# The head of a gated-mix kernel: x0's second half in token order, wk's first rows on SyncE's queue, ScalarE's loads behind its table load

## The chip, the core and the metric

One core of one Trainium2 chip. The metric is the device time of one execution in microseconds. The kernel before takes 261.64 us (median of 3 runs, 261.2 to 262.14).

## The reference, cut to what matters

x has 2048 tokens of 512 features in bf16. Two branches read it and a gate mixes them.

```python
x = A_x
g = _sigmoid((x * gate_w).sum(-1, keepdims=True))     # one gate value per token
a = _A_ref(x, A_wq, A_wk, A_wv, A_wo, A_beta)          # attention with a compressive memory
b = _B_ref(x, B_w_gate, B_w_up, B_w_down)              # gelu(x @ w_gate) * (x @ w_up) @ w_down
return g * a + (1 - g) * b
...
# _A_ref: 32 heads of 16 features, 4 segments of 512 tokens, in order
for s in range(N):
    qs, ks, vs = (q[:, :, s].copy(), k[:, :, s].copy(), v[:, :, s].copy())
    logits = jnp.einsum('bhqd,bhkd->bhqk', qs, ks) * scale + mask
    p = _softmax(logits, axis=-1)
    a_dot = jnp.einsum('bhqk,bhkd->bhqd', p, vs)
    ...
    o = g * a_mem + (1.0 - g) * a_dot
    ...
    M = M + jnp.einsum('bhld,bhle->bhde', pk, vs)
```

## The kernel before, in words

The four segments of 512 tokens are worked on one behind another, but their pieces are interleaved. Every piece is a task: a projection (K, Q, V), a block of attention, a tile of the gate (G), up (U) or down (D) products, an eviction, a DMA. The order of the tasks on each engine is written out by hand in ORDER (five strings, one for each of TensorE, ScalarE, VectorE, GpSimd and SyncE). A small planner, `Sched.schedule`, walks these orders with estimated durations. All that it decides is which of the four PSUM banks psW0 to psW3 a task takes; for the first loads it reads the estimated landing times from the table LANDING. `Emitter` then derives the semaphore waits from what each instruction reads and writes, and writes each engine's instructions in the order given.

The change lies in the head, before segment 0 can be projected.

- Segment 0's tokens come in two loads, x0_0 and x0_1, of 256 tokens each, into `xin` (four rows of 512 features in each partition; a part of the tile hT1, so the profile calls them hT). Before, both lay as "(p a) d": partition p holds tokens 2p and 2p+1 of the half, which are neighbours in memory, so each partition's piece is one run of 2 KB.
- wk, wq and wv are cut into pieces of rows: wk0 and wk1 (128 rows, 128 KB each), wk2 (256 rows, 256 KB), wq0, wq1, wv0 and wv1 (256 rows each). SyncE issues x0_0, x0_1, wk2, wq1, wv1, then wg0 (the first half of w_gate, 896 KB), and segment 1's transposing loads x1_0 to x1_3 with the gate's weights gwb and beta among them. ScalarE issues wk0, wk1, wq0 and wv0. They stand in its order behind `tload`, a one-element exponential which makes the table of functions load.
- TensorE begins with seven warm-up matmuls `warm0` to `warm6` of 512 columns, whose results nobody reads. Then come the transposes of x0_0 (`x0t0a_0`, `x0t0c_0`, `x0t0b_0`, `x0t1_0`: eight matmuls of 128 columns against an identity, into PSUM), evicted to `xT[0]` by VectorE and ScalarE (`x0ev...`). The K projection is cut into eight matmuls of 256 columns for each of four tiles: `.0` reads wk0 and the first half of the tokens, `.1` wk1 and the first half, `.2` and `.3` the same weights and the second half, `.4` to `.7` wk2. The order on TensorE is: transposes of x0_0, the four `.0`, transposes of x0_1, the four `.1`, then `.2`, `.3`, `.4` and so on; then the Q projection of segment 0 (16 matmuls of 512 columns), the last three of K, and the first tiles of G, which need wg0.
- The evictions of the transposes undo the token order: with tokens 2p and 2p+1 in partition p, the copy writes every second column of `xT[0]`.
- The gate of segment 0: `gmul0` multiplies `xin` by gwb on VectorE, `gsum0_0` to `gsum0_3` sum each row over the 512 features into columns 12 to 15 of `glog`, and four small DMAs on SyncE, `gl00` to `gl11`, move them to where each token's value belongs in columns 0 to 3, since the tokens' order in `xin` isn't that of the output tiles. `gexs0` on ScalarE takes the exponential of columns 0 to 3.

Of the kernel before, what the change touches and what calls it, by code (L numbers as in the profile page):

```python
# [13 lines left out]
ALU = mybir.AluOpType  # L14
# [24 lines left out]
LANDING = {  # L39
    "x0_0": 3.8, "w_wk0": 4.15, "x0_1": 5.2, "w_wk1": 5.7, "w_wk2": 6.6, "w_wq0": 7.0, "w_wq1": 8.4, "w_wv0": 9.2,  # L40
    "w_wv1": 10.2, "w_wg0": 12.2, "x1_0": 12.9, "w_gwb": 13.2, "x1_1": 13.8, "w_beta": 14.1, "x1_2": 14.4, "x1_3": 14.8,
# [53 lines left out]
    "act": (  # L95
# [349 lines left out]
def mm_t(n):  # L445
    return max(0.026, n / 2363.0)
# [19 lines left out]
def _build(es, nc, A_x, A_wq, A_wk, A_wv, A_wo, A_beta, B_w_gate, B_w_up, B_w_down, gate_w, out):  # L466
# [71 lines left out]
    def task(name, eng, instrs, **kw):  # L538
        return S.add(Task(name, {eng: instrs}, **kw))
# [55 lines left out]
    def wdma(key, eng, dst, src, nbytes, nonc=False, issue=0.5, reads=()):  # L595
        rank[0] -= 20000.0 if rank[0] > 1.0e5 else 20.0
        dma("w_" + str(key), eng, lambda: dst, lambda: src, list(reads), [("w", key)], nbytes, bias=rank[0],
            nonc=nonc, issue=issue)
# [25 lines left out]
    for u in range(2):  # L624
        rank[0] -= 20000.0
        dma(f"x0_{u}", SP, lambda u=u: xin[:, 2 * u:2 * u + 2, :],
            lambda u=u: A_x[0, u * 256:(u + 1) * 256, :].rearrange("(p a) d -> p a d", p=P), [],
            [("hT", 1, 2 * u + a) for a in range(2)], 250000, bias=rank[0], issue=0.5)
        for wkey, i, dst, src in wloads[u:u + 1] if u == 0 else wloads[1:]:
            wdma((wkey, i), SP if (wkey, i) in (("wk", 2), ("wq", 1), ("wv", 1)) else ACT, dst, src, 250000,  # L630
                 issue=0.5)
    wdma(("wg", 0), SP, wg[:, :, 0:half], wgr[:, :, 0:half], 790000)
# [7 lines left out]
    for i in range(7):  # L640
        gw = Grp(banks)
        task(f"warm{i}", PE, [Instr(lambda e, gw=gw: e.matmul(
            gw.f32()[:, :], ones[:, 0:128], ones[:, :], start=True, stop=True),
            [], [gw.key], mm_t(512))], grp=gw, bias=5000.0 - i)
    XB = XALL.bitcast(BF)
    for nm, u, k0, nk, c0, aa in (("0a", 0, 0, 1, 0, (0,)), ("0c", 0, 0, 1, 3584, (1,)), ("0b", 0, 1, 1, 1024, (0, 1)),
# [9 lines left out]
            for k in range(nk) for i, a in enumerate(aa)])  # L656
        dst = xT[0][:, k0:k0 + nk, 256 * u:256 * u + 256].rearrange("p k (c a) -> p k a c", a=2)[:, :, aa[0]:aa[-1] + 1, :]
        wr = [("xT", 0, k0 + k, u) if na == 2 else ("xT", 0, k0 + k, u, aa[0]) for k in range(nk)]
# [117 lines left out]
    def prep(s):  # L776
# [35 lines left out]
        if s > 0:  # L812
# [4 lines left out]
            ALU.mult), xkeys + [("w", "gwb")], xkeys, 1.32)])  # L817
        gl, gk = (glog[:, 12:16], ("glog", 3)) if s == 0 else (glog[:, s4], ("glog", s))
        for a in range(4):
            S.add(Task(f"gsum{s}_{a}", {  # L820
                ACT: [Instr(lambda e, a=a: e.activation(xt[:, a, :], xt[:, a, :], ACTF.Copy,
                                                        accum_out=gl[:, a:a + 1]),
                            [("gprod", s)] + xkeys, [gk + (a,), ("gjunk", s, a)], 0.64)],
                DVE: [Instr(lambda e, a=a: e.tensor_reduce(gl[:, a:a + 1], xt[:, a, :], AXX, ALU.add),
                            [("gprod", s)] + xkeys, [gk + (a,), ("gjunk", s, a)], dve_t(512))]}))
        if s == 0:
            for h in range(2):
                for a in range(2):
                    dma(f"gl{h}{a}", SP, lambda h=h, a=a: glog[a:P:2, h:4:2],
                        lambda h=h, a=a: glog[64 * h:64 * h + 64, 12 + a:16:2],  # L830
                        [gk + (c,) for c in (a, 2 + a)], [("glog", 0, h, a), ("glog", 0, 2 + h, a)], 60000, nonc=True)
        exp_task(ph, f"gexs{s}", [Instr(lambda e: e.activation(exs[:, s4], glog[:, s4], ACTF.Exp),
                                        [("glog", s, a) + u for a in range(4)
                                         for u in (((0,), (1,)) if s == 0 else ((),))], [("exs", s)], 0.25)])
        task(f"gts{s}", DVE, [
# [442 lines left out]
```

## Time and the profile before

| | |
|---|---|
| median of 3 runs | 261.64 us |
| the profiled execution's own time | 261.51 us |
| its span, first to last instruction | 260.3 us |
| granted TensorE clock over it | 1.00 |
| instructions | 10390 |
| DMA packets, bytes | 33100, 18.43 MB |
| HBM read, written | 9.84 MB, 2.10 MB |

The profile is one execution, taken by the hardware profiler. Times are microseconds from the start of the span unless they are marked ns. PE is TensorE's matmuls and PEld its weight loads, which overlap them; DVE is VectorE, ACT ScalarE, POOL GpSimd, SP SyncE. A name with a q behind it (SPq, ACTq) is that engine's sequencer issuing DMAs, which is not counted as busy time. Matmuls are pipelined and their ends are modelled, so a matmul's length is longer than the distance to the next one. A DMA's time to landing runs from its issue to the event that it has arrived. q1 is the queue that SyncE issues to, q10 the one of ScalarE. An arrow in brackets names what ended the idle time before an instruction. A share of the DMA engines over 1 means packets that overlap in time.

### The profile page before, as it was taken

How to read it: one execution, taken by the hardware profiler on the slowest of the kernel's cores; microseconds unless marked ns; L12 is line 12 of the kernel's file. 1: busy time of each engine (PE TensorE's matmuls, PEld its weight loads, DVE VectorE, ACT ScalarE, POOL GpSimd, SP SyncE). 2: the span in 40 equal slices, each digit the busy share in tenths (PEclk: the TensorE clock that was granted, in tenths of full speed). 3: DMA queues.
4: the chain of work that ended last, by engine and by line, in shares of the span. 5: the costliest groups of instructions: out<-in, count | busy, mean ns of one | idle time of the engine just before them, and what ended most of it. 6: DMA issues, size and time to landing. Idle time of an engine off the chain costs nothing.

```text
span 260.3 us, 10390 instructions
## 1 busy us (share of the span) xinstructions
PE 252.8 (97%) x4645; PEld 126.8 (49%) x4670; DVE 186.7 (72%) x346; ACT 211.3 (81%) x192; POOL 105.9 (41%) x260
## 2 busy tenths in 40 slices
PE   7999999999999999999999999999999999999996
PEld 3644445445554664534454563454455445454454
DVE  2398889998998338898987317889898602688574
ACT  4799999999998887979868967889985878777721
POOL 8216767814007264263810251445280044327320
DMA  7962212997013272070004023102001200420002
GB/s 220 309 180 42 59 30 59 252 358 149 3 23 61 44 106 63 12 115 3 3 4 102 4 63 73 33 4 87 0 6 23 81 5 0 108 61 3 3 3 83
DMA packets 33100, 18.43 MB, mean 71 GB/s; under 512 B 21152, under 2 KB 32800, under 8 KB 33056
## 3 DMA queue, kind: packets, MB, share of 16 engines
q1 hardware_dynamic: 32080, 16.96, 27.4%
q10 hardware_dynamic: 976, 0.82, 0.9%
q8 instruction: 36, 0.59, 0.9%
q14 instruction: 8, 0.07, 0.1%
HBM read 9.84 MB, written 2.10 MB: 46 GB/s over the span
## 4 chain that ended last, share of the span: by engine, by line
PE 92%; ACT 3%; DMA 2%; issue 2%; DVE 1%; SPq 0%; ACTq 0%
PE psW L544 33%; PE psW L546 25%; PE psW L1104 14%; PE psXALL L936 9%; PE psW L984 5%; DMA hT<-in_A_x_dram 2%; PE psXALL L546 2%; PE psW L992 1%; ACT ptl L942 1%; PE psXALL L544 1%; ACT pt L942 1%; PE psXALL L855 1%; PE psW L902 1%; DVE hT L1083 0%; PE psXALL L653 0%
## 5 line engine op out<-in xcount | busy, mean ns | idle before, releaser
L942 ACT ACTIVATE pt<-psXALL 128x2048 bf16<-128x2048 f32 x64 | 120.2, 1877 | 24.5 <-PE psXALL L936 23.5
L945 POOL TENSOR_SCALAR_AFFINE_SELECT pt<-pt 128x256 bf16<-128x256 bf16 x128 | 56.1, 448 | 90.1 <-ACT pt L942 85.3
L945 POOL TENSOR_SCALAR_AFFINE_SELECT ptl<-ptl 128x512 bf16<-128x512 bf16 x32 | 23.9, 747 | 48.6 <-ACT ptl L942 47.0
L1083 DVE TENSOR_TENSOR hT<-psW,hT 128x512 bf16<-128x512 f32 x56 | 37.2, 683 | 8.9 <-PE psW L544 6.7
L1104 PE MATMUL psW<-wd,hT 32*128 32x512 bf16 x576 | 35.0, 374 | 0.0
L544 PE MATMUL psW<-xT,wg 128*128 128x512 bf16 x121 | 29.8, 380 | 1.0 <-issue 0.6
L544 PE MATMUL psW<-xT,wu 128*128 128x512 bf16 x118 | 29.4, 380 | 1.3 <-issue 1.3
L998 DVE STREAM_TRANSPOSE tb<-psW 128x512 f32<-128x512 f32 x32 | 22.3, 705 | 8.7 <-PE psW L992 8.5
L936 PE MATMUL psXALL<-qT,kpad 32*128 32x320 bf16 (+3 forms) x512 | 25.6, 272 | 0.4 <-ACT ptl L942 0.2
L546 PE MATMUL psW<-xT,wu 128*32 128x512 bf16 x392 | 24.6, 380 | 0.0
L1133 DVE TENSOR_SCALAR ost<-psW,omgt 128x512 bf16<-128x512 f32 x11 | 8.0, 746 | 23.1 <-PE psW L544 21.9
L1104 PEld LDWEIGHTS psW<-wd,hT 32*128 32x128 bf16 x576 | 18.8, 93 | 10.6
L546 PE MATMUL psW<-xT,wg 128*32 128x512 bf16 x384 | 22.9, 380 | 0.0
L1067 ACT ACTIVATE hT<-psW 128x512 bf16<-128x512 f32 x28 | 15.5, 598 | 7.3 <-PE psW L546 7.1
L936 PEld LDWEIGHTS psXALL<-qT,kpad 32*128 32x128 bf16 x512 | 8.6, 92 | 22.7 <-ACT pt L942 15.9
L984 PE MATMUL psW<-pt,vaug 128*17 128x192 bf16 (+3 forms) x512 | 19.3, 273 | 0.0
L544 PEld LDWEIGHTS psW<-xT,wg 128*128 128x128 bf16 x128 | 11.5, 98 | 14.5 <-issue 1.5
L544 PEld LDWEIGHTS psW<-xT,wu 128*128 128x128 bf16 x126 | 11.2, 98 | 14.3 <-issue 2.1
L984 PEld LDWEIGHTS psW<-pt,vaug 128*17 128x17 bf16 x512 | 12.3, 91 | 10.0 <-issue 0.6
L942 ACT ACTIVATE ptl<-psXALL 128x2048 bf16<-128x2048 f32 x8 | 15.0, 1877 | 1.6 <-PE psXALL L936 1.6
L842 POOL COPY exsT<-exs 32x4 f32<-32x4 f32 x64 | 14.0, 219 | 3.8
L546 PEld LDWEIGHTS psW<-xT,wu 128*32 128x32 bf16 x392 | 10.1, 97 | 9.5 <-issue 0.8
(126 smaller groups left out, 379.8 us busy)
## 6 DMA issues: line engine op xcount, KB each, us to landing
out_dram<-ost SPq DMA_DIRECT2D x15, 128.0 KB, 1.8
wg<-in_B_w_gate_dram SPq DMA_DIRECT2D x2, 896.0 KB, 7.7
wu<-in_B_w_up_dram SPq DMA_DIRECT2D x2, 896.0 KB, 6.7
wd<-in_B_w_down_dram SPq DMA_DIRECT2D x2, 896.0 KB, 7.2
phkt<-in_A_x_dram SPq DMA_DIRECT2D x3, 512.0 KB, 3.9
vlow<-vaug SPq DMA_DIRECT2D x8, 136.0 KB, 2.7
hT<-in_A_x_dram SPq DMA_DIRECT2D x2, 256.0 KB, 3.6
wo<-in_A_wo_dram SPq DMA_DIRECT2D x1, 512.0 KB, 5.6
```

What stands on the lines that cost most here:

```text
L544: return e.matmul(view(), lhsT, rhs, start=first, stop=last)
L546: r = e.matmul(view()[c:c + 32, :], lhsT[:, c:c + 32], rhs, start=first, stop=last, tile_position=(0, c))
L842: cross = task(f"exsT{s}", POOL, [Instr(lambda e, g=g, c=c: e.tensor_copy(exsT[sl][32 * g:32 * g + 32, c:16:4], exs[32 * c:32 * c + 32, s4 ...
L936: instrs.append(Instr(lambda e, g=g, lhs=lhs, rhs=rhs, c0=c0, ncol=ncol: e.matmul(X[g][:, c0:c0 + ncol], lhs(32 * g), rhs(32 * g), start=T ...
L942: exp_task(s, f"exp{s}_{t}{name}", [Instr(lambda e: e.activation(dst[:], XALL[:, :].rearrange("p (g c) -> p g c", g=4), ACTF.Exp, scale=AT ...
L945: task(f"msk{s}_{t}{name}", POOL, [Instr(lambda e, view=view, pat=pat, base=base: e.affine_select(out=view, in_=view, compare_op=ALU.is_ge ...
L984: instrs.append(Instr(lambda e, t=t, q=q, kb=kb, slot=slot, c0=c0: e.matmul(gp.f32()[32 * q:32 * q + 17, 128 * kb + 64:512], Vaug[sl][:, k ...
L998: task(f"pvt{s}_{t}_{j}", DVE, [Instr(lambda e: e.transpose(Tb[:, j, :], gp.f32()[:, :]), [gp.key], [("Tb", j)], 0.71)], grp=gp)
L1067: lambda e, g=g, ft=ft, s=s: e.activation(hT[s % 2][:, ft, :], g.f32()[:, :], ACTF.Gelu_apprx_tanh),
L1083: task(f"Um{s}_{ft}", DVE, [Instr(lambda e, g=g, ft=ft: e.tensor_tensor(hT[sl][:, ft, :], g.f32()[:, :], hT[sl][:, ft, :], ALU.mult), [g.k ...
L1104: return Instr(lambda e: e.matmul(gs[tile].f32()[:, :], a[32 * r:32 * r + 32, :], b[32 * r:32 * r + 32, :], start=False, stop=False, tile_ ...
L1133: DVE: [Instr(lambda e: e.tensor_scalar(ost[:], g.f32()[:, :], omgt[:, gt:gt + 1], None, ALU.mult), rd, wr, dve_t(512, ap=True))]}, grp=g))
```

## The change

Six edits, and with them the line numbers behind them move by up to three.

- x0_1 is laid out as "(a p) d": partition p holds tokens p and 128 + p of the half. They aren't neighbours in memory, so each partition's piece is two runs of 1 KB. x0_0 stays as it was.
- The evictions of x0_1's transposes therefore write whole runs of columns of `xT[0]`, no longer every second one.
- wk0 moves from ScalarE's order to SyncE's, between x0_0 and x0_1.
- wk1, wq0 and wv0, still on ScalarE, now read the word that `tload` writes, so the first of them waits until `tload` is done and the two behind it follow.
- `warm6` has 128 columns instead of 512.
- The gate's sums for x0_1's tokens go straight into columns 2 and 3 of `glog`. The four small moves remain, but each takes one column instead of two and waits for one sum instead of two.

The estimated landing times in LANDING are set anew too; the PSUM banks that the planner gives out come out the same, and so does the order of everything else.

```diff
     "act": (
-        "tload w_wk0 w_wk1 w_wq0 w_wv0 x0ev0c_0 x0ev0b_0 x0ev0b_1 x0ev1_1 K0_0even K0_1ev K0_2ev kl0_01 pke0_0 Q0_1ev "
+        "tload w_wk1 w_wq0 w_wv0 x0ev0c_0 x0ev0b_0 x0ev0b_1 x0ev1_1 K0_0even K0_1ev K0_2ev kl0_01 pke0_0 Q0_1ev "
...
     "sp": (
-        "x0_0 x0_1 w_wk2 w_wq1 w_wv1 w_wg0 x1_0 w_gwb x1_1 w_beta x1_2 x1_3 w_wg1 gl00 gl11 Vlo0_1 gl10 gl01 pkT0_1 "
+        "x0_0 w_wk0 x0_1 w_wk2 w_wq1 w_wv1 w_wg0 x1_0 w_gwb x1_1 w_beta x1_2 x1_3 w_wg1 gl00 gl11 Vlo0_1 gl10 gl01 "
...
         dma(f"x0_{u}", SP, lambda u=u: xin[:, 2 * u:2 * u + 2, :],
-            lambda u=u: A_x[0, u * 256:(u + 1) * 256, :].rearrange("(p a) d -> p a d", p=P), [],
+            lambda u=u: A_x[0, u * 256:(u + 1) * 256, :].rearrange(("(p a) d -> p a d", "(a p) d -> p a d")[u], p=P), [],
             [("hT", 1, 2 * u + a) for a in range(2)], 250000, bias=rank[0], issue=0.5)
         for wkey, i, dst, src in wloads[u:u + 1] if u == 0 else wloads[1:]:
-            wdma((wkey, i), SP if (wkey, i) in (("wk", 2), ("wq", 1), ("wv", 1)) else ACT, dst, src, 250000,
-                 issue=0.5)
+            late = (wkey, i) in (("wk", 1), ("wq", 0), ("wv", 0))
+            wdma((wkey, i), ACT if late else SP, dst, src, 250000, issue=0.5, reads=[("stmp",)] if late else ())
...
     for i in range(7):
         gw = Grp(banks)
-        task(f"warm{i}", PE, [Instr(lambda e, gw=gw: e.matmul(
-            gw.f32()[:, :], ones[:, 0:128], ones[:, :], start=True, stop=True),
-            [], [gw.key], mm_t(512))], grp=gw, bias=5000.0 - i)
+        n = 128 if i == 6 else 512
+        task(f"warm{i}", PE, [Instr(lambda e, gw=gw, n=n: e.matmul(
+            gw.f32()[:, 0:n], ones[:, 0:128], ones[:, 0:n], start=True, stop=True),
+            [], [gw.key], mm_t(n))], grp=gw, bias=5000.0 - i)
...
-        dst = xT[0][:, k0:k0 + nk, 256 * u:256 * u + 256].rearrange("p k (c a) -> p k a c", a=2)[:, :, aa[0]:aa[-1] + 1, :]
+        dst = xT[0][:, k0:k0 + nk, 256 * u:256 * u + 256].rearrange(
+            ("p k (c a) -> p k a c", "p k (a c) -> p k a c")[u], a=2)[:, :, aa[0]:aa[-1] + 1, :]
...
-        gl, gk = (glog[:, 12:16], ("glog", 3)) if s == 0 else (glog[:, s4], ("glog", s))
+        col = [12, 13, 2, 3] if s == 0 else [4 * s + a for a in range(4)]
+        gks = [("glog", c // 4, c % 4) for c in col]
...
-                    dma(f"gl{h}{a}", SP, lambda h=h, a=a: glog[a:P:2, h:4:2],
-                        lambda h=h, a=a: glog[64 * h:64 * h + 64, 12 + a:16:2],
-                        [gk + (c,) for c in (a, 2 + a)], [("glog", 0, h, a), ("glog", 0, 2 + h, a)], 60000, nonc=True)
+                    dma(f"gl{h}{a}", SP, lambda h=h, a=a: glog[a:P:2, h:h + 1],
+                        lambda h=h, a=a: glog[64 * h:64 * h + 64, 12 + a:13 + a],
+                        [gks[a]], [("glog", 0, h, a)], 60000, nonc=True)
```

More of the change, by code (lines that the diff above doesn't have):

```diff
@@ L39 @@
 LANDING = {
-    "x0_0": 3.8, "w_wk0": 4.15, "x0_1": 5.2, "w_wk1": 5.7, "w_wk2": 6.6, "w_wq0": 7.0, "w_wq1": 8.4, "w_wv0": 9.2,
+    "x0_0": 3.5, "w_wk0": 3.85, "x0_1": 4.65, "w_wk1": 4.6, "w_wk2": 5.7, "w_wq0": 6.3, "w_wq1": 7.6, "w_wv0": 8.4,
     "w_wv1": 10.2, "w_wg0": 12.2, "x1_0": 12.9, "w_gwb": 13.2, "x1_1": 13.8, "w_beta": 14.1, "x1_2": 14.4, "x1_3": 14.8,
@@ L821, in prep @@
                 ACT: [Instr(lambda e, a=a: e.activation(xt[:, a, :], xt[:, a, :], ACTF.Copy,
[L822 to L825, printed above, removed]
+                                                        accum_out=glog[:, col[a]:col[a] + 1]),
+                            [("gprod", s)] + xkeys, [gks[a], ("gjunk", s, a)], 0.64)],
+                DVE: [Instr(lambda e, a=a: e.tensor_reduce(glog[:, col[a]:col[a] + 1], xt[:, a, :], AXX, ALU.add),
+                            [("gprod", s)] + xkeys, [gks[a], ("gjunk", s, a)], dve_t(512))]}))
         if s == 0:
@@ L828, in prep @@
                 for a in range(2):
-                    dma(f"gl{h}{a}", SP, lambda h=h, a=a: glog[a:P:2, h:4:2],
-                        lambda h=h, a=a: glog[64 * h:64 * h + 64, 12 + a:16:2],
-                        [gk + (c,) for c in (a, 2 + a)], [("glog", 0, h, a), ("glog", 0, 2 + h, a)], 60000, nonc=True)
+                    dma(f"gl{h}{a}", SP, lambda h=h, a=a: glog[a:P:2, h:h + 1],
+                        lambda h=h, a=a: glog[64 * h:64 * h + 64, 12 + a:13 + a],
+                        [gks[a]], [("glog", 0, h, a)], 60000, nonc=True)
         exp_task(ph, f"gexs{s}", [Instr(lambda e: e.activation(exs[:, s4], glog[:, s4], ACTF.Exp),
                                         [("glog", s, a) + u for a in range(4)
-                                         for u in (((0,), (1,)) if s == 0 else ((),))], [("exs", s)], 0.25)])
+                                         for u in (((0,), (1,)) if (s, a) in ((0, 0), (0, 1)) else ((),))], [("exs", s)], 0.25)])
         task(f"gts{s}", DVE, [
```

6 rows, old and new, of the table ORDER are left out of this document.

## The prediction

> **What bounds the kernel now.** I read the page first, for the engine that sets the end.
>
> ```profile
> span 260.3 us, 10390 instructions
> PE 252.8 (97%) x4645; PEld 126.8 (49%) x4670; DVE 186.7 (72%) x346; ACT 211.3 (81%) x192; POOL 105.9 (41%) x260
> PE 92%; ACT 3%; DMA 2%; issue 2%; DVE 1%; SPq 0%; ACTq 0%
> ```
>
> TensorE is busy for 97% of the span and is 92% of the chain that ended last. So the change, which touches only the head, is worth what it moves TensorE's stream there, if nothing later takes it back. Then I read the chain of waits over the first 16 us (start, length, what).
>
> ```profile
> 1.27 4.26 DMA hT<-in_A_x_dram
> 5.53 0.05 issue
> 5.57 0.62 PE psXALL L653 x8
> 6.19 2.73 PE psW L544 x25
> 8.97 3.40 PE psXALL L544 x15
> 12.38 1.19 PE psW L544 x7
> ```
>
> The DMA is x0_1, x's second 256 tokens: issued at 1.27, landed at 5.53. From 5.57 on, the chain is TensorE almost without a break. Next the timeline of the head (start, length, engine, line; in brackets the idle time before it and what ended it), with the warm-up's group of the by-shape view behind it.
>
> ```profile
> 0.81 1.28 ACT L617 ACT_TABLE_LOAD   x1 [0.81 <-PEq L1263]
> 0.85 3.15 PE L642 MATMUL psW<-const-bfloat16-1.0 128*128 128x512 bf16 x7 [0.85 <-PEq L1263]
> 0.87 0.89 ACTq L581 DMA_DIRECT2D wk<-in_A_wk_dram  x2
> 1.72 0.43 SPq L581 DMA_DIRECT2D wk<-in_A_wk_dram  x1
> 2.10 0.20 ACT L617 ACTIVATE stmp<-const-bfloat16-1.0 128x1 f32<-128x1 bf16 x1
> 3.82 0.47 PEld L653 LDWEIGHTS psXALL<-ident,hT 128*128 128x128 bf16 x8 [0.73 <-DMA hT<-in_A_x_dram]
> 3.83 0.64 PE L653 MATMUL psXALL<-ident,hT 128*128 128x128 bf16 x8
> 4.58 0.60 PE L544 MATMUL psW<-xT,wk 128*128 128x256 bf16 x4
> 5.57 0.62 PE L653 MATMUL psXALL<-ident,hT 128*128 128x128 bf16 x8 [0.40 <-DMA hT<-in_A_x_dram]
> 5.90 0.45 DVE L661 COPY xT<-psXALL 128x256 bf16<-128x256 bf16 x1 [0.66 <-PE psXALL L653]
> 5.98 2.67 PEld L544 LDWEIGHTS psW<-xT,wk 128*128 128x128 bf16 x25
> 12.43 0.64 PEld L544 LDWEIGHTS psW<-xT,wg 128*128 128x128 bf16 x4
> ...
> L642 PE MATMUL psW<-const-bfloat16-1.0 128*128 128x512 bf16 x7 | 3.1, 625 | 0.9 <-PEq L1263 0.9
> ```
>
> There are two gates. The first transposes start at 3.83, when two things end together: the seven warm-up matmuls (six steps of (3.15 - 0.625)/6 = 0.42 us, so the last starts at 3.37 and is through the array by about 3.80) and x0_0's landing. The second transposes wait 0.40 us for x0_1. Last I read the DMA view, for the landings (us from issue, one row of each load's own window) and for the packets.
>
> ```profile
> hT<-in_A_x_dram SPq DMA_DIRECT2D x1, 256.0 KB, 3.0
> wk<-in_A_wk_dram ACTq DMA_DIRECT2D x1, 128.0 KB, 3.2
> ...
> hT<-in_A_x_dram SPq DMA_DIRECT2D x1, 256.0 KB, 4.3
> ...
> wk<-in_A_wk_dram SPq DMA_DIRECT2D x1, 256.0 KB, 5.0
> wk<-in_A_wk_dram ACTq DMA_DIRECT2D x1, 128.0 KB, 4.5
> ...
> wg<-in_B_w_gate_dram SPq DMA_DIRECT2D x1, 896.0 KB, 9.0
> ```
>
> So x0_0 lands at 0.81 + 3.0 = 3.8, wk0 at 4.1, wk1 (issued about 1.3) at 5.8, wk2 at 6.7, and wg0, issued at 3.22, at 12.2. The packets of SyncE's queue (q1) and ScalarE's (q10), as packets, MB and share of the 16 engines, from 1.6 to 2.8, to 3.2 and to 4.4 us; then two stretches of the windows view, whose last figure is GB/s:
>
> ```profile
> q1 hardware_dynamic: 92, 0.19, 76.2%
> q10 hardware_dynamic: 2, 0.00, 0.5%
> ...
> q1 hardware_dynamic: 138, 0.26, 68.8%
> q10 hardware_dynamic: 64, 0.06, 11.5%
> ...
> q1 hardware_dynamic: 299, 0.53, 67.6%
> q10 hardware_dynamic: 251, 0.23, 24.2%
> ...
> 2.40:2.80 0.40, 0.40 (x2) 1.00 0.67 138
> 3.20:4.00 0.80, 0.80 (x5) 1.00 1.13 385
> ```
>
> ScalarE's wk0, issued at 0.87, has moved two packets by 2.8, though SyncE's x0_0, issued 0.06 us before it, has moved 92. And between 2.4 and 2.8 the engines move 138 GB/s where they move 385 soon after: x0_0 is running out and nothing else is there yet. That hole is worth 0.4 x (1 - 138/385) = 0.26 us of transfer.
>
> **The change, part by part.** *The seventh warm-up* shrinks from 512 to 128 columns: a quarter of 0.42, so TensorE is free at 3.37 + 0.11 = 3.48 instead of 3.80. That is 0.32 us at most, and only if x0_0 is there.
>
> *wk0 on SyncE's queue, ahead of x0_1.* SyncE now issues x0_0 at 0.81, wk0 at 1.27 and x0_1 at about 1.70, one issue (0.43) later than before; wk2, wq1, wv1, wg0 and the x1 loads slip by the same 0.43, but their data stands behind megabytes, so I cost the slip of the issues alone at nothing. In bytes the order up to x0_1's end stays: x0_0, wk0, x0_1, 640 KB. What goes is the hole. Also ScalarE's 0.06 MB no longer mixes into x0_0's end: 0.06 MB at 385 GB/s is 0.16 us. So x0_0 lands at 3.66 (bounds: 3.48, below which the warm-up rules, and 3.82, unchanged). TensorE takes 1.34 us from the first transposes to being ready for the second ones (3.83 to 5.57 - 0.40 = 5.17), so it is ready at about 5.0 (bounds 4.82 and 5.17).
>
> *x0_1's landing.* Its last byte, the 640th KB (0.655 MB), passed at about 4.1 (202 GB/s up to 3.2, from the 0.32 MB above, then 385); without the hole 3.85. From last byte to landing x0_0 took 3.82 - 3.2 = 0.6, x0_1 itself 5.53 - 4.1 = 1.4. So it lands between 4.45 and 5.27. If ScalarE's wk1 (128 KB, 0.34 us) gets in before it, up to 5.6. I take 5.05, nearer to its own row than to x0_0's, for the engines are as full then as before. The transposes start at 5.09 instead of 5.57: **0.48 us earlier** (bounds 0 and 0.75, the latter 5.57 - 4.82 with no wait left).
>
> *1-KB packets.* The shares above give 0.676 x 16 x 2.8 / 299 = 0.101 us for a packet of q1 (1.8 KB in the mean) and 0.043 for one of q10 (0.9 KB): per byte the short ones are no dearer. Cost nothing; upper bound, if x0_1 took as long a packet as q1's for half the bytes, 16 packets an engine x 0.101 against 0.81, 0.8 us more. I hold to the q10 row, since its packets are 1-KB rows like these.
>
> *Evictions of the second half.* VectorE's copy of 256 elements (0.45) now writes one contiguous run; between 0.15 us less and no change, and either way beside TensorE's four matmuls at 5.98, so nothing on the path.
>
> *ScalarE's loads behind its table load.* wk1 is issued no earlier than 2.10 + 0.20 + a hop, about 2.37, instead of 1.3; wq0 and wv0 follow at 2.83 and 3.3, until 3.8, and behind them on ScalarE stands only the eviction of x0_0, which needs the transposes (4.17 before). wk1 must be in by the time the second transposes are through, 5.98 - 0.48 = 5.50. First in its queue it should do as wk0 did, 3.2 us: 5.57; but much of wk0's 3.2 was waiting (two packets by 2.8), so I take 5.2 and no wait. Upper bound: its old 4.5, landing at 6.87.
>
> *wk2 and wg0.* wk2 is needed by the tenth matmul after 5.50 (25 in 2.67, 0.107 each): 6.57; it landed at 6.72 and without the hole lands at 6.46. No wait; 0.15 if the hole stays. wg0 is needed at 12.43 - 0.48 = 11.95; 12.22 - 0.26 = 11.96. I charge 0.05 (bounds 0 and 0.27).
>
> *The gate's columns.* The four small moves take one column instead of two and wait for one sum each.
>
> ```profile
> L580 SPq DMA_DIRECT2D glog<-glog x4: 596/612/709, 19.7 to 23.0; - x4
> L832 ACT ACTIVATE exs<-glog x1: 197/197/197, 27.1 to 27.1; 128x4 f32<-128x4 f32 x1
> DMA to landing us min/median/max: 1.8/1.8/2.1
> ```
>
> The last landed by 25.1, two microseconds before its reader at 27.1: nothing.
>
> The sum: 0.48 - 0.05 = 0.43 us less, on the profiled execution's 261.51 (span 260.3 and 1.2 around it): 261.08, say **261.1**. That execution lies 0.13 below the median of 261.64.
>
> The Trainium skill, "DMA: Bandwidth & Descriptors", section "Issuing engines are not separate DMA queues", says that loads of several engines share the same 16 DMA engines, and that a second issuer saves only issuing time. It speaks against this change, and what it would make of the time is the rival "x0_1 keeps its 4.26 us" below. The packet rows agree with it only in part: 1.9 us after its issue ScalarE's load had moved 2 packets, when SyncE's had moved 92.
>
> **The rivals.** *Both waits go (0.30).* x0_0 lands by 3.48 and x0_1 by 4.82: gain 0.75, 260.76. For it: the hole sits just ahead of x0_0's last packets, and without ScalarE's load the lag may fall to x0_0's 0.6. Against: x0_0 must gain 0.34, more than the hole.
>
> *The wait moves on (0.09).* wk2 (6.72) or wg0 (12.22) keeps its landing; TensorE then stands at 12.43 - 0.2, a gain of 0.2 or less: 261.3 to 261.6. For it: the bytes ahead of both are the same. Against: the hole.
>
> *x0_1 keeps its 4.26 us (0.05).* Moving wk0 buys no transfer and costs x0_1 one issue: 1.70 + 4.26 = 5.96, the second transposes at 6.00, 0.43 later than before, 261.94. For it: the bytes ahead of x0_1 don't change. Against: its 4.26 us ends with bytes that passed at 4.1, not with its issue.
>
> *wk1 is late, slower (0.10).* Issued at 2.37, with its old 4.5 us, it lands at 6.87, and the K matmuls that began at 5.98 begin at 6.91: 0.93 later, 262.4. It decides from a landing at 5.94 on. For it: 4.5 us was queueing among four loads in flight, and now x0_1 and wk2 are in flight too. Against: 128 KB at half of 385 GB/s take 0.7 us, and no load is ahead of it in its queue.
>
> *The clock comes late, slower (0.03).* The warm-up matmuls ran at 0.42 us each, while fifteen of 512 columns later take 3.40, 0.23 each. If x0_0 isn't there at 3.48, TensorE idles where it was busy; should the step to the fast clock come 3 us (3.82 - 0.82) later for that, half of them is lost: 1.5 us, 263.0. Against: 0.3 us of idling in 3.
>
> The Trainium skill, "TensorE: Matmul & The Clock Gate", Part 1, says that the clock is released after a busy window of about 3.4 us, and that the window runs freely, not from the first matmul. By that rule the step comes at different moments in different executions, with or without this change; the trace of one execution can't show it.
>
> **How the numbers follow.** Forecast 0.43, with a range of its own from 260.8 to 261.4; both waits gone 0.30; moved on 0.09; x0_1 keeps its 4.26 us 0.05; slower 0.13. A measurement of this kernel tells about 0.3%, 0.8 us, from no change; from 261.64 that is 260.86 and 262.42. So faster 0.30 (the first rival), same 0.57 (the forecast, the wait moved on, x0_1's latency kept), slower 0.13. The range reaches from 260.6, a little under the first rival for the spread of the runs (0.9 us among three), to 262.0, which leaves out most of the late wk1.
>
> **What would show it.** Right: the first transposes at 3.5 to 3.7, the second at about 5.1 with at most 0.1 us of waiting, no hole in the transfer rate at 2.4, TensorE at wg's first weights near 12.0. Wrong: x0_1 landing past 5.4; a wait for wk ahead of the 25 matmuls (late wk1) or inside them (wk2); a wait at 12 us for wg; a first run of eight transposes well over its 0.64 us, as a slow clock would have it.

## The result, and the profile after

The changed kernel is slower: 263.27 us (median of 22 runs, 261.85 to 266.6) against 261.64 (22 runs of the kernel before, 261.16 to 262.36). The ratio is 1.0067, with a 95% interval from 1.0048 to 1.0086. The ratios here and in the table below leave out one run of after (266.6) and one of b_wait (267.36), each over 1.5% above the fastest of its kernel, so they aren't the quotients of the medians. The profiled execution took 263.15 us, 1.64 more than the one of before (261.51).

The page of the kernel after, first the span, then busy time of the engines, then the shares of the chain that ended last:

```profile
span 261.9 us, 10414 instructions
PE 257.2 (98%) x4670; PEld 127.2 (49%) x4670; DVE 186.5 (71%) x346; ACT 211.2 (81%) x192; POOL 106.2 (41%) x260
PE 96%; DMA 2%; ACT 1%; issue 0%; ACTq 0%
```

TensorE still sets the end, so the loss has to be ahead of its stream. The chain of waits over the first 16 us (start, length, what):

```profile
0.82 1.28 ACT L617
2.12 0.21 ACT stmp L617
2.35 5.27 DMA wk<-in_A_wk_dram
7.67 2.90 PE psW L544 x25
10.57 3.45 PE psXALL L544 x16
14.02 1.19 PE psW L544 x7
```

Before, the chain began with x0_1. Now it begins with ScalarE's table load, goes over the wait that the change added to wk1, 5.27 us to its landing at 7.62, and from there through TensorE. The timeline of the same stretch (start, length, engine, line; in brackets the idle time before it and what ended it):

```profile
1.27 0.41 SPq L581 DMA_DIRECT2D wk<-in_A_wk_dram  x1
1.73 0.43 SPq L581 DMA_DIRECT2D hT<-in_A_x_dram  x1
2.20 0.47 SPq L581 DMA_DIRECT2D wk<-in_A_wk_dram  x1
2.35 0.40 ACTq L581 DMA_DIRECT2D wk<-in_A_wk_dram  x1
3.75 1.03 PE L654 MATMUL psXALL<-ident,hT 128*128 128x128 bf16 x8
6.57 0.62 PE L654 MATMUL psXALL<-ident,hT 128*128 128x128 bf16 x8 [0.93 <-DMA hT<-in_A_x_dram]
7.66 2.63 PEld L544 LDWEIGHTS psW<-xT,wk 128*128 128x128 bf16 x25 [0.64 <-DMA wk<-in_A_wk_dram]
10.30 3.23 PEld L544 LDWEIGHTS psXALL<-xT,wq 128*128 128x128 bf16 x16
14.08 0.64 PEld L544 LDWEIGHTS psW<-xT,wg 128*128 128x128 bf16 x4
```

There are two waits where there was one. The second transposes start at 6.57 (5.57 before), 1.00 later, for x0_1. Before, the 25 K matmuls' weight loads followed 0.41 behind those transposes; now they follow 1.09 behind, 0.68 more, for wk1. Q's first weight load, 2.67 behind K's before, is now 2.64 behind. Its row of the kernel before:

```profile
8.65 3.23 PEld L544 LDWEIGHTS psXALL<-xT,wq 128*128 128x128 bf16 x16
```

So 1.00 + 0.68 - 0.03 = 1.65 us at Q (8.65 before, 10.30 after), and still 14.08 - 12.43 = 1.65 at wg's first weights.

The landings in the DMA view (us from issue; each row from a window around its own issue) and, behind them, the packets from 3.2 to 4.2 us as packets, MB and share of the 16 engines:

```profile
hT<-in_A_x_dram SPq DMA_DIRECT2D x1, 256.0 KB, 4.8
wk<-in_A_wk_dram SPq DMA_DIRECT2D x1, 256.0 KB, 5.7
wk<-in_A_wk_dram ACTq DMA_DIRECT2D x1, 128.0 KB, 5.3
...
q1 hardware_dynamic: 225, 0.22, 75.4%
q10 hardware_dynamic: 2, 0.00, 0.6%
```

The same packet rows of the kernel before:

```profile
q1 hardware_dynamic: 130, 0.24, 70.0%
q10 hardware_dynamic: 143, 0.13, 38.9%
```

x0_1 lands at 1.73 + 4.8 = 6.53, wk1 at 2.35 + 5.27 = 7.62, wk2 at 2.20 + 5.7 = 7.9. ScalarE's queue moves two packets by 4.2 us, 1.8 us from its first issue (2.35 to 4.19); in the kernel before it was 1.9 (0.87 to 2.77). Until then only SyncE's queue moves data, and it moves no more than it did beside the other one (0.22 MB against 0.24). The windows view from 3.2 to 4.8 us shows it as a rate (length, TensorE's busy time, granted clock, DMA share, GB/s), first of after:

```profile
3.20:4.80 1.60, 1.53 (x12) 1.00 0.71 193
```

and then of before:

```profile
3.20:4.80 1.60, 1.49 (x13) 1.00 1.06 361
```

The hole that the prediction read in the kernel before, 138 GB/s from 2.4 to 2.8 us, is closed in after; the low stretch lies behind it. The row of after:

```profile
2.40:2.80 0.40, 0.40 (x2) 1.00 0.80 305
```

### The profile page after: what moved, and what is told of

Its sections match the earlier page's. It is cut to its first block, busy times and chain, and to the rows that moved or that the text cites. A ratio compares the mean times of both kernels' runs of the same rounds, so it can differ in the third digit from the quotient of the medians.

```text
span 261.9 us, 10414 instructions
## 1 busy us (share of the span) xinstructions
PE 257.2 (98%) x4670; PEld 127.2 (49%) x4670; DVE 186.5 (71%) x346; ACT 211.2 (81%) x192; POOL 106.2 (41%) x260
## 4 chain that ended last, share of the span: by engine, by line
PE 96%; DMA 2%; ACT 1%; issue 0%; ACTq 0%
PE psW L544 36%; PE psW L546 26%; PE psW L1107 14%; PE psXALL L939 9%; PE psW L987 6%; DMA wk<-in_A_wk_dram 2%; PE psXALL L546 2%; PE psW L995 1%; PE psXALL L544 1%; ACT ptl L945 1%; PE psXALL L858 1%; PE psW L905 1%; ACT L617 0%; ACT obf L1170 0%; ACT stmp L617 0%
## 5 line engine op out<-in xcount | busy, mean ns | idle before, releaser
L544 PE MATMUL psW<-xT,wg 128*128 128x512 bf16 x128 | 31.3, 380 | 0.0
L544 PE MATMUL psW<-xT,wu 128*128 128x512 bf16 x126 | 31.2, 380 | 0.0
```

The costliest lines, as they stand in the source:

```text
L544: return e.matmul(view(), lhsT, rhs, start=first, stop=last)
```

## The experiments

All the numbers of the eighteen kernels in one place. "Q" is the start of Q's first weight load in the profiled execution, "rest" that execution's time less Q.

| kernel | median us (lowest to highest, runs) | ratio to before, 95% | profiled | Q | rest |
|---|---|---|---|---|---|
| before | 261.64 (261.16 to 262.36, 22) | | 261.51 | 8.65 | 252.86 |
| after | 263.27 (261.85 to 266.6, 22) | 1.0067 [1.0048, 1.0086] | 263.15 | 10.30 | 252.85 |
| a_nowait | 263.15 (262.24 to 264.33, 7) | 1.0056 [1.0033, 1.0080] | 262.35 | 9.46 | 252.89 |
| a_wk0back | 262.81 (261.77 to 265.58, 12) | 1.0056 [1.0032, 1.0081] | 261.82 | 8.95 | 252.87 |
| a_runs | 263.46 (261.98 to 265.04, 12) | 1.0071 [1.0047, 1.0096] | 262.18 | 9.27 | 252.91 |
| a_warm | 263.44 (262.96 to 264.86, 6) | 1.0074 [1.0052, 1.0097] | 263.67 | 10.82 | 252.85 |
| b_wait | 265.99 (263.25 to 267.36, 6) | 1.0145 [1.0110, 1.0181] | 267.36 | 14.46 | 252.90 |
| b_wk0 | 262.42 (262.14 to 265.14, 12) | 1.0047 [1.0024, 1.0069] | 262.46 | 9.61 | 252.85 |
| b_token | 261.91 (261.54 to 262.22, 11) | 1.0006 [0.9996, 1.0015] | 261.57 | 8.68 | 252.89 |
| b_warm | 261.61 (261.09 to 262.06, 11) | 0.9998 [0.9987, 1.0009] | 261.63 | 8.77 | 252.86 |
| a_queues_back | 261.58 (261.36 to 262.14, 11) | 1.0009 [0.9998, 1.0020] | 262.13 | 9.28 | 252.85 |
| b_ident | 261.77 (261.12 to 262.17, 12) | 1.0003 [0.9992, 1.0015] | 261.12 | 8.26 | 252.86 |
| one_queue | 261.97 (261.62 to 262.46, 11) | 1.0014 [1.0004, 1.0024] | 262.12 | 9.12 | 253.00 |
| a_swap | 263.26 (263.14 to 263.47, 5) | 1.0062 [1.0047, 1.0077] | 263.42 | 10.54 | 252.88 |
| b_wait_all | 262.30 (261.99 to 262.91, 12) | 1.0030 [1.0019, 1.0040] | 262.32 | 9.43 | 252.89 |
| a_wv0first | 263.78 (263.19 to 264.22, 4) | 1.0081 [1.0061, 1.0101] | 263.59 | 10.76 | 252.83 |
| c_ident_warm | 261.89 (261.20 to 262.55, 12) | 1.0009 [0.9997, 1.0021] | 261.92 | 9.08 | 252.84 |
| c_ident_warm_token | 262.00 (261.32 to 262.67, 12) | 1.0010 [0.9997, 1.0023] | 261.39 | 8.39 | 253.00 |

The rest is 252.83 to 253.00 in all eighteen. Whatever the head loses or gains goes to the end unchanged. What decides lies ahead of Q: the waits for x0_1, wk1, wk2 or wq and, in some traces, matmuls that still run at the slow pace of the warm-up (the eight second transposes take 1.06 us in a_queues_back, 0.62 in the kernel before). A profiled execution can lie more than a microsecond off its kernel's median (those of a_wk0back and a_runs are among their fastest), so times are read from the runs and places from the traces, and one trace doesn't give the size of an effect.

### From after, one part undone

*a_nowait*: ScalarE's loads wait for nothing, wk0 stays on SyncE.

```diff
-            late = (wkey, i) in (("wk", 1), ("wq", 0), ("wv", 0))
+            late = (wkey, i) in ()
```

> The changed kernel, but ScalarE's wk1, wq0 and wv0 no longer wait for the table load (wk0 stays on SyncE, x0_1 in token order, warm6 short). Theory Q (late queue: the first packet of ScalarE's queue comes 1.7 us after its issue in both traces, so an issue at 2.35 instead of 1.3 makes wk1 the last gate): wk1 lands before 6.0, the 25 K matmuls start at about 6, and the time is 261.0 to 261.8. Theory P (x0_1's 1-KB pieces in token order move slowly: 215 GB/s from 3.2 to 4.0 us against 385 before): x0_1 still lands near 6.5 and the time stays above 262. Theory C (the short warm-up lets the clock come late or drop): no change, 263, with runs of 264 to 265 as before.

Measured: still 0.56% slower than before; the 261.0 to 261.8 of theory Q was missed. Its loads are issued in the order x0_0 0.82, wk1 0.87, wk0 1.28, wq0 1.30, x0_1 1.73, wv0 1.78, wk2 2.20, and they land in exactly that order: 3.8, 4.0, 4.4, 5.1, 6.0, 7.5 and 7.9. The transfer rate from 3.2 to 4.8 us is back at 380 GB/s. What follows: the added wait isn't the only thing that costs. Without it, ScalarE's wk1 and wq0 are issued ahead of x0_1, and x0_1 lands 0.5 later than before; wk2 comes late next.

*a_wk0back*: wk0 goes back to ScalarE and waits for nothing; the three loads behind it keep the wait.

```diff
-        "tload w_wk1 w_wq0 w_wv0 ...
+        "tload w_wk0 w_wk1 w_wq0 w_wv0 ...
-        "x0_0 w_wk0 x0_1 w_wk2 ...
+        "x0_0 x0_1 w_wk2 ...
```

> The changed kernel with wk0 back on ScalarE, issued ahead of the wait at 0.87; wk1, wq0 and wv0 still wait for the table load. Theory Q: ScalarE's queue has been started by wk0, so wk1 lands earlier than 7.6, about 6.3 to 6.9, and the time is 261.8 to 262.5. Theory P: x0_1 in token order is still slow and the time stays near 263. Theory C: no change.

Measured: 0.56% slower than before in the runs. In its trace x0_1, issued at 1.27 again, lands at 4.8 and wk1, issued at 2.35, at 6.3, with a wait of 0.68 us; the rate is 380 GB/s. What follows: either of the two queue edits costs about as much as both together.

*a_runs* and *a_warm*: x0_1 in 2-KB runs again, with its evictions and gate columns; and all seven warm-up matmuls at 512 columns again.

```diff
-(("(p a) d -> p a d", "(a p) d -> p a d")[u], p=P)
+("(p a) d -> p a d", p=P)
...
-        n = 128 if i == 6 else 512
+        n = 512
```

> The changed kernel, but x0_1 again in 2-KB runs, with its evictions and gate columns as before the change. Theory P: the transfer rate from 3.2 to 4.4 us is back above 330 GB/s, x0_1 lands by 5.5 and the time is near 261.5. Theory Q: x0_1 may land earlier, but wk1 still lands past 7, the 25 K matmuls still start past 7, and the time stays above 262.5. Theory C: no change.

> The changed kernel with the seventh warm-up matmul back at 512 columns. Theory C: the times close up to one group near 262 or below, none of 264 or more. Theories P and Q: median and spread as the changed kernel's, 262.2 to 265, within 0.3 us of its median.

Measured: 263.46 and 263.44, as slow as after. The low rate stays as well (248 and 167 GB/s from 3.2 to 4.8 us). What follows: the 1-KB packets and the short warm-up aren't the cause. The two traces also show how much wk1's landing varies. In a_runs, among its fastest executions, wk1 lands at 6.0 and nothing waits for it; in a_warm it lands at 8.1, in after at 7.6. In all three it is issued at about 2.35, 0.15 behind wk2 (rates of 248, 167 and 193 GB/s).

### From before, one part added

*b_wait*: the added wait alone; wk0 stays on ScalarE.

```diff
+            late = (wkey, i) in (("wk", 1), ("wq", 0), ("wv", 0))
-            wdma(... issue=0.5)
+            wdma(... issue=0.5, reads=[("stmp",)] if late else ())
```

> The kernel before with one part added: ScalarE's wk1, wq0 and wv0 wait for the table load; wk0 is issued on ScalarE ahead of them as before. Theory Q: wk1 is issued at about 2.35 and lands past 6.3; the 25 K matmuls start 0.3 us or more later and the time rises by 0.3 to 1 us over the kernel before. Theory P: no change, within 0.2 us.

Measured: 1.45% slower, the worst of all, where theory Q had 0.3 to 1 us. Its profiled execution is the slowest of its six runs, so its sizes are an upper end. Its timeline, with the row of Q:

```profile
9.49 5.24 PE L544 MATMUL psW<-xT,wk 128*128 128x256 bf16 x25 [3.78 <-DMA wk<-in_A_wk_dram]
14.46 1.50 PEld L544 LDWEIGHTS psXALL<-xT,wq 128*128 128x128 bf16 x8
```

its landings (wk2, issued at 1.73; wq1, at 2.2; wk1, at 2.35):

```profile
wk<-in_A_wk_dram SPq DMA_DIRECT2D x1, 256.0 KB, 4.5
wq<-in_A_wq_dram SPq DMA_DIRECT2D x1, 256.0 KB, 6.6
wk<-in_A_wk_dram ACTq DMA_DIRECT2D x1, 128.0 KB, 7.1
```

and the windows view in the wait and behind it (the last three figures are granted clock, DMA share and GB/s):

```profile
5.70:7.40 1.70, 0.01 (x1) 1.00 1.00 302
7.50:9.40 1.90, 0.00 (x0) 0.50 1.03 365
9.40:10.40 1.00, 0.91 (x5) 0.50 1.06 382
```

wk1 lands at 9.4, behind wk2 (6.2) and wq1 (8.8), which were issued ahead of it: 128 KB wait for 512 KB that are needed later. TensorE stands for 3.78 us, and about halfway through that wait the granted clock falls to 0.50: the 25 matmuls take 5.24 instead of 2.89. The transfer rate is high here (359 GB/s from 3.2 to 4.8 us), so here it is the order, and the clock behind it. The other five runs took 263.25 to 266.61.

*b_wk0*: wk0 moves to SyncE, and nothing waits.

```diff
-        "tload w_wk0 w_wk1 w_wq0 w_wv0 ...
+        "tload w_wk1 w_wq0 w_wv0 ...
-        "x0_0 x0_1 w_wk2 ...
+        "x0_0 w_wk0 x0_1 w_wk2 ...
```

> The kernel before with one part added: wk0 on SyncE between x0_0 and x0_1, ScalarE's wk1, wq0 and wv0 issued from 0.87 on without a wait. Theory Q: wk1 is issued at 0.87, moves from 2.6 on and lands ahead of x0_1; the time is that of the kernel before within 0.3 us, or a little less. Theory P: the same. If it is 0.5 us slower, the move of wk0 itself is the cause (x0_1 issued 0.43 later).

Measured: 0.47% slower. The landings of wq0 (issued at 1.30), x0_1 (1.73) and wk2 (2.19):

```profile
wq<-in_A_wq_dram ACTq DMA_DIRECT2D x1, 256.0 KB, 3.9
hT<-in_A_x_dram SPq DMA_DIRECT2D x1, 256.0 KB, 4.3
wk<-in_A_wk_dram SPq DMA_DIRECT2D x1, 256.0 KB, 5.8
```

and its timeline:

```profile
6.05 0.90 PE L654 MATMUL psXALL<-ident,hT 128*128 128x128 bf16 x8 [0.23 <-DMA hT<-in_A_x_dram]
8.06 1.53 PEld L544 LDWEIGHTS psW<-xT,wk 128*128 128x128 bf16 x15 [0.30 <-DMA wk<-in_A_wk_dram]
9.61 3.23 PEld L544 LDWEIGHTS psXALL<-xT,wq 128*128 128x128 bf16 x16
```

x0_1 keeps its 4.3 us and lands as much later as it was issued later, behind wq0 (5.2), whose issue now comes ahead of it. wk2 is late as well, inside the 25 matmuls. The second transposes still run at the slow pace (0.90 instead of 0.62), which is a part of the loss in this trace. Two things changed with this edit, not one: x0_1 is issued 0.46 later, and ScalarE's wk1 and wq0 now go ahead of it. Q starts 0.96 later than before, and the profiled execution takes 0.95 more.

*b_token* and *b_warm*: x0_1 in token order with its evictions and gate columns; and the short seventh warm-up.

```diff
+            ...rearrange(("(p a) d -> p a d", "(a p) d -> p a d")[u], p=P)
...
+        n = 128 if i == 6 else 512
```

> The kernel before with one part added: x0_1 in token order in 1-KB pieces, with its evictions and gate columns. Theory P: x0_1 lands past 6, the rate from 3.2 to 4.4 us falls under 300 GB/s, and the time rises by 0.5 us or more. Theory Q: no change or a small gain, within 0.3 us.

> The kernel before with one part added: the seventh warm-up matmul has 128 columns. Theories P and Q: no change, within 0.2 us, since the first transposes wait for x0_0 at 3.8. Theory C: times of 264 and more among the runs, or a median 0.3 us or more above the kernel before.

Measured: 1.0006 and 0.9998, neither to be told from no change. In b_token's trace x0_1 lands at about 5.55, in the kernel before at 5.53: no price for 1-KB packets that could be told from nothing.

*a_queues_back* is after with both queue edits undone, so before with these two parts together.

> The changed kernel with both queue edits undone: wk0 back on ScalarE and no wait; token order and short warm-up stay. If the loss lies in the queue edits alone, the time is that of the kernel before within 0.2 us (token order alone and the short warm-up alone made no difference); if the two harmless parts hurt together, it is 0.4 us or more above. A gain of 0.3 us or more would mean that the short warm-up pays once x0_1 lands earlier.

Measured: 1.0009, with an interval from 0.9998 to 1.0020. What follows: the loss is that of the queue edits, to within this interval, and the other parts bring no gain of their own.

### Order of issue or a low transfer rate

Two theories were left for what the queue edits do. One (O where an expectation gives it a letter): the first loads land in the order in which they are issued, whichever queue they are on, so an urgent load that is issued later stands behind others. The other (D): while ScalarE's queue is silent, less is moved in all, and everything is late, whatever the order.

*b_ident*: before, but wk1, wq0 and wv0 wait for GpSimd's identity matrix, which is there earlier than `tload`; wk1 is issued at 1.57 instead of 1.30, still ahead of wk2.

```diff
+                 reads=[("c", "ident")] if late else ())
```

> The kernel before, with ScalarE's wk1, wq0 and wv0 waiting for GpSimd's identity (done at 1.54) instead of the table load: wk1 is issued at about 1.65, still ahead of wk2's 1.72 on SyncE, so the order of issue is that of the kernel before. Theory O (the first loads land in the order of their issue, whichever queue; wk1's loss is that wk2 and wq1 are issued ahead of it): wk1 lands by 6.1 and the time is within 0.4 us of the kernel before. Theory L (any delay of ScalarE's loads counts, since its queue needs 1.7 us from issue to first packet): wk1 lands 0.3 to 0.4 later than 5.8, at 6.1 to 6.2, and about 0.2 us is lost. Theory T (waiting itself, or the table load, is what hurts): as with the wait on the table load, 263 to 266.

Measured: 1.0003. Its landing of wk1:

```profile
wk<-in_A_wk_dram ACTq DMA_DIRECT2D x1, 128.0 KB, 3.5
```

and its row of Q in the timeline:

```profile
8.26 3.23 PEld L544 LDWEIGHTS psXALL<-xT,wq 128*128 128x128 bf16 x16
```

wk1 lands at 5.1 though it waited, and x0_1 at 4.7 instead of 5.53. That x0_1 is early isn't shown to come from the wait: in b_warm, with the loads of the kernel before, it lands at 5.0. This wait of 0.27 us, with the order of issue kept, costs nothing that the runs can tell. This execution's Q is the earliest of all, but the runs show no gain.

*b_wait_all*: before, with the wait of the change on both queues' later loads (wk1, wq0 and wv0 on ScalarE; wk2, wq1 and wv1 on SyncE), so that wk2 is issued beside wk1 (2.33 and 2.34) and wq1 behind it (2.77).

```diff
+            late = (wkey, i) in (("wk", 1), ("wq", 0), ("wv", 0), ("wk", 2), ("wq", 1), ("wv", 1))
```

> The kernel before, with the loads of both queues behind x0_0, wk0 and x0_1 waiting for the table load (ScalarE's wk1, wq0, wv0 and SyncE's wk2, wq1, wv1 and all behind them), so that nothing is issued ahead of wk1 that was behind it. Theory O (the first loads land in the order of their issue): wk1 lands before 6.6, hundreds of KB earlier than the 9.44 of the wait on ScalarE alone, and the time is 261.5 to 262.7. Theory L (late loads on ScalarE's queue cost by themselves): wk1 lands past 7.5 and the time stays above 264.

Measured: 0.30% slower than before where b_wait is 1.45% slower, though more loads wait. wk1's landing:

```profile
wk<-in_A_wk_dram ACTq DMA_DIRECT2D x1, 128.0 KB, 4.4
```

and, in the timeline, the matmuls that read it:

```profile
6.79 2.90 PE L544 MATMUL psW<-xT,wk 128*128 128x256 bf16 x25 [1.10 <-DMA wk<-in_A_wk_dram]
```

Issued at the same moment as in b_wait, wk1 lands at 6.7 instead of 9.4, now that wk2 and wq1 aren't issued ahead of it. The wait of SyncE's loads, and with it the order of issue, is the one edit between the two, so the order is what b_wait pays most for. The 0.3% that is left goes with the late issue: TensorE still stands 1.10 us.

*one_queue*: before, with all first loads on SyncE's queue in the order in which they are needed.

```diff
-        "x0_0 x0_1 w_wk2 w_wq1 w_wv1 ...
+        "x0_0 w_wk0 x0_1 w_wk1 w_wk2 w_wq0 w_wq1 w_wv0 w_wv1 ...
```

> The kernel before, with all the first loads on SyncE in the order in which TensorE needs them: x0_0, wk0, x0_1, wk1, wk2, wq0, wq1, wv0, wv1, wg0. Theory O: they land in that order; x0_1 at 5.3 to 5.8 and wk1 at 5.8 to 6.2; the time is 261.4 to 262.2. Theory D (the transfer rate falls to 150 to 255 GB/s from 3.2 to 4.8 us when SyncE's queue alone feeds the engines): x0_1 lands past 6.3 and wk1 past 7, and the time is above 263. If the low rate comes from ScalarE's queue being started late, it is gone here, since that queue isn't used: 340 GB/s or more from 3.2 on.

Measured: 1.0014, from 1.0004 to 1.0024. The loads land in their order, x0_1 at 5.6, wk1 at 6.5. Of theory D the low rate came true, the late x0_1 and the 263 did not; the 340 GB/s of its last sentence was missed too. The windows view:

```profile
3.20:4.80 1.60, 1.60 (x11) 1.00 0.81 188
```

and the row of Q in the timeline:

```profile
9.12 3.23 PEld L544 LDWEIGHTS psXALL<-xT,wq 128*128 128x128 bf16 x16
```

The low rate is there with ScalarE's queue not used at all, so it isn't the start of that queue that slows the transfer. But with the loads in the order of need it costs only 0.14%. That is the nearest to the rule of the Trainium skill, "DMA: Bandwidth & Descriptors", section "Issuing engines are not separate DMA queues", that a second issuer saves only issuing time: in the time of the kernel it nearly holds, in the rate of these 1.6 us it doesn't (188 GB/s with one issuer, 361 with two).

*a_swap*: after, with wk1 on SyncE behind x0_1, and wk2 as the first of ScalarE's waiting loads.

```diff
-        "tload w_wk1 ...
+        "tload w_wk2 ...
-        "x0_0 w_wk0 x0_1 w_wk2 ...
+        "x0_0 w_wk0 x0_1 w_wk1 ...
```

> The changed kernel with wk1 and wk2 exchanged: wk1 on SyncE behind x0_1, wk2 first on ScalarE behind the table load. The order of issue is then the order of need. Theory O: wk1 lands within 0.5 us of x0_1 and the 25 K matmuls no longer wait for it at their start; what is left is a wait for wk2 inside them; the time is 261.8 to 262.6. Theory D: the rate is still 150 to 255 GB/s from 3.2 to 4.8 us, x0_1 still lands past 5.7, and the time stays above 262.5, though with fewer runs of 264 and more.

Measured: 263.26, as slow as after; the time that the order alone would give, 261.8 to 262.6, was missed. x0_1 lands at 6.0, wk1 at 7.5 though it is now issued ahead of wk2, wk2 at 9.0. The windows view:

```profile
3.20:4.80 1.60, 1.50 (x11) 1.00 0.59 180
```

So putting the order right for wk1 doesn't mend the kernel after. Nor is a low rate enough to explain it. one_queue issues the same four first loads at the same times (0.82, 1.27, 1.73 and about 2.2) and moves no more (188 GB/s), yet its x0_1 lands 0.4 earlier and its wk1 1.0 earlier. What the traces show to be different is whose bytes move. The packets from 3.2 to 4.8 us, of a_swap:

```profile
q1 hardware_dynamic: 215, 0.21, 40.9%
q10 hardware_dynamic: 77, 0.08, 18.0%
```

and of one_queue:

```profile
q1 hardware_dynamic: 221, 0.30, 81.3%
```

In a_swap a part of the same total goes to ScalarE's loads, wk2 and wq0, which are needed later. In one_queue all of it goes to the loads in the order of need. That fits the difference, but the token order and the short warm-up differ as well (neutral elsewhere), and no run has this alone.

*a_wv0first*: after, with wv0 issued by ScalarE at 0.87 without a wait, so that its queue moves data early; only wk1 and wq0 wait.

```diff
-        "tload w_wk1 w_wq0 w_wv0 ...
+        "tload w_wv0 w_wk1 w_wq0 ...
-            late = (wkey, i) in (("wk", 1), ("wq", 0), ("wv", 0))
+            late = (wkey, i) in (("wk", 1), ("wq", 0))
```

> The changed kernel, but ScalarE issues wv0 at once (0.87) and only wk1 and wq0 wait for the table load. Theory D (the low rate comes when SyncE's queue alone issues in the first two microseconds): the rate from 3.2 to 4.8 us is 330 GB/s or more; wv0's 256 KB now go ahead of x0_1, which still lands near 6, and wk1 near 7; time 262.5 to 264.5. If the rate is still 150 to 255 GB/s there, theory D falls.

Measured: 263.78. The windows view:

```profile
3.20:4.80 1.60, 0.93 (x7) 1.00 1.09 315
```

The rate rises from 193 to 315 GB/s, a little under the 330 expected, and part of the hole moves behind it (219 GB/s from 4.8 to 5.6). But the early bytes are wv0's, the last needed: wk1 lands at 7.3 only. An early second queue brings the rate back, and with the wrong load on it the time is no better. x0_0 is late here too (4.3), so TensorE waits 0.67 for it, and the slow pace of the start reaches into the 25 K matmuls (3.72 instead of 2.90).

*c_ident_warm* and *c_ident_warm_token* put together what had cost nothing, to beat both kernels: b_ident with the short warm-up, and both with the token order.

> The kernel before, with ScalarE's wk1, wq0 and wv0 waiting for GpSimd's identity (done at 1.54) and the short seventh warm-up matmul. If the gap between x0_0's landing at 3.5 and the end of the warm-up is worth something, the first transposes start at 3.5 to 3.6 and the time is 261.0 to 261.4, 0.2 to 0.5 us under the kernel before; if the clock step or a later wait takes it back, the time is the kernel before's within 0.2 us.

> As c_ident_warm, with x0_1 in token order in 1-KB pieces too. Token order alone made no difference, so the same as c_ident_warm within 0.2 us; if 1-KB pieces hurt once x0_1 is the only load of its kind in flight, 0.3 us or more slower.

Measured: 1.0009 and 1.0010, both intervals with 1 inside. In both traces the first transposes start at 4.0, so the early start that was hoped for isn't there. No version was found that beats the kernel before.

## Why the prediction was wrong, step by step

- *TensorE's stream carries the head to the end one to one.* Right: 1.65 us at Q, 1.64 in the time.
- *The seventh warm-up.* The first transposes came at 3.75 instead of 3.83; the 3.66 of the prediction was near. In the runs it is worth nothing (b_warm).
- *x0_1's landing: the step that failed.* The prediction took 5.05, on two assumptions: "I cost the slip of the issues alone at nothing", and that the order in bytes fixes the landing once the hole is closed. It landed at 6.53, 1.48 later. The slip isn't free. In the ten traces in which SyncE issues x0_1 at 1.27 it lands between 4.7 and 5.6; in the eight in which wk0 stands ahead and it is issued at 1.73, it lands between 5.6 and 6.5, on the mean 1.0 later for 0.46 us of issue. The lowest of the eight is one_queue's, where only x0_0 and wk0 go ahead and no second queue is used; in the others ScalarE's loads go ahead of it or move beside it, so the slip isn't the whole of it. That was the rival "x0_1 keeps its 4.26 us", held at 0.05, and even it was too small for after, where x0_1 takes 4.8. The hole at 2.4 us did close (305 GB/s), but from 3.2 to 4.8 us the rate fell to 193, which no term of the prediction had. One reading was off as well: x0_1's last byte passed at about 4.3 in the kernel before, not 4.1 (SyncE's queue had moved x0_0's and x0_1's 0.52 MB only then), because ScalarE's bytes were mixed in. And the 5.53 that it started from is itself one draw of 4.7 to 5.6.
- *wk1: the second step that failed.* "5.2 and no wait" was argued from wk1's place at the head of its own queue. It landed at 7.62. That the place among all loads counts is shown by b_wait against b_wait_all. In after itself wk2 is issued only 0.15 ahead and lands behind wk1 (7.9), and a_swap, with wk1 ahead of wk2, is no faster; there the late issue meets the low rate, and how much of the delay each has stays open. The rival "wk1 is late" had the mechanism of the late issue and the right first sentence for it (x0_1 and wk2 in flight), at a chance of 0.10 and at too low a price: 6.87 and a loss of 0.93 at the K matmuls, where 1.68 was measured, of which 1.00 is x0_1's. Together, 1.48 + 0.68 less the 0.05 charged for wg0 and 0.03 at Q is 2.08, and the profiled execution lies 2.07 above the forecast.
- *wk2 and wg0.* Right that neither is waited for, but only because TensorE came later: wk2 landed at 7.9 instead of 6.46, before its reader at about 7.66 + 10 x 0.107 = 8.7.
- *1-KB packets, evictions, the gate's columns.* Right: nothing (b_token). The upper bound of 0.8 us for the packets wasn't touched.
- *The clock.* The sign of a slow clock was there, eight transposes in 1.03 us instead of 0.64, but b_wk0, with its full warm-up, shows 1.03 in the same place. In after's trace the eight are through long before x0_1, the second ones take 0.62 again, and it cost nothing. That fits the free-running window which the prediction cited from the Trainium skill. What no term had is a clock that falls again later. Of after's 22 runs eight show a granted clock of 0.994 or 0.987 over the whole execution, and they take 264.58 to 266.6; the fourteen at 1.00 take 261.85 to 264.66, with a median of 262.23. No run of the kernel before whose clock is on record shows less than 1.00. As an estimate, 0.994 over 264 us is 1.6 us lost, half speed for some 3 us. So the fourteen lie 0.6 us above the kernel before in the median, and the 263.27 lies between two groups of runs. The rival "the clock comes late" had 263.0, close to that by luck: its mechanism was another.

What stays open: why one issuer alone moves so little from 3.2 to 4.8 us. In the five kernels in which only SyncE issues in the first 2.3 us (after, a_runs, a_warm, a_swap, one_queue) the rate is 167 to 248 GB/s; in the others it is 302 to 391. It isn't the queue's own limit, for in one_queue it moves 362 GB/s from 5.6 to 7.0 us. Open too is why a_swap loses and one_queue hardly does, with the same first four issues and the same rate. Nor do the parts add up: the wait alone costs 1.45%, with the two neutral parts beside it 0.56% (a_wk0back). In the two traces wk1 lands behind wq1 in the one and ahead of it in the other, though it was issued 0.1 to 0.2 us behind it in both; whether that is chance or the packets' shape wasn't tried. The longest runs of after weren't traced. That their clock fell is on record; that it fell in a wait at the head, as in b_wait's trace, is an argument and not a reading.

## What to carry to other kernels

Where the first loads of a kernel are a burst on several queues, write down one list of all of them by time of issue, and read each landing from its place in that list, not from its place in its own queue. A load that is made to wait loses its place to everything that is issued meanwhile, and a load put ahead of another costs that one its issue slot and lets the other queue's loads in. Before such an edit is costed at nothing, ask which load with a later reader is now ahead. And where TensorE is made to stand, read the granted clock of every run, not only of the traced one.

## What the runs showed of the hardware that was not expected

- The loads of the first 3 us land in the order of issue across the two queues: in a_nowait all seven, in the other traces with neighbours changing places at most (in after wk1, issued 0.15 us behind wk2, lands 0.3 ahead of it).
- ScalarE's queue takes about 1.9 us from its first issue to its first packet (0.87 to 2.77 before, 2.35 to 4.19 after; 1.4 in a_swap), SyncE's about 1.0 (0.82 to 1.83). The 1.7 of two expectations is a little short. An urgent load on ScalarE's queue pays the longer one.
- In b_wait's trace TensorE stood from 5.7 to 9.5 us, and the granted clock was 1.00 up to 7.4 and 0.50 from 7.5 on; the next 25 matmuls took 5.24 us instead of 2.89. The Trainium skill, "TensorE: Matmul & The Clock Gate", Part 1, says that an idle window of about 3.4 us brings the slow clock back. The trace differs: the clock fell after some 1.8 us without a matmul. Waits of 1.26 us (a_warm), 1.10 (b_wait_all) and 0.93 (after) left it at 1.00 in their traces.
